# Sinkhorn normalisation re-laid: one (batch, head, source block) per partition, row sums by a block matrix on TensorE

## The chip, the core and the metric

The kernel runs on one core of one Trainium2 chip. The metric is the device time in microseconds (us) of one execution, as the median of several runs. Work is done by TensorE (PE, with its weight loads shown apart as PEld), VectorE (DVE), ScalarE (ACT) and GpSimd (POOL); SyncE (SP) issues plain transfers, POOL issues the loads that cast from float32 to bfloat16, and all transfers share 16 DMA engines.

## What is computed

The reference, cut to what matters here:

```
# q, k, v: (4, 8, 768, 64); sort_net: (4, 8, 8, 8); block = 96
P = sort_net
for _ in range(5):
    P = exp(P - max(P, axis=-1))
    P = P / (sum(P, axis=-1) + 1e-9)     # over source blocks j, for each target block i
    P = P / (sum(P, axis=-2) + 1e-9)     # over target blocks i, for each source block j
k_sorted, v_sorted = P applied to the 8 blocks of k and of v, for each (batch, head)
attn = softmax(q_block @ k_sorted_block.T / 8)       # inside each block of 96 rows
x = (attn @ v_sorted_block), heads side by side      # 3072 x 512
out = (s * relu(x @ w_in)**2 + b) @ w_out            # 512 -> 2048 -> 512
```

There are 32 (batch, head) pairs, so sort_net is 32 matrices of 8 x 8, or 256 rows (batch, head, i) of 8 numbers.

## The kernel before

**Tiles and stages.** The output's 3072 rows are made as eight tiles t of 384 rows; tile t is half of batch t//2. For each tile the attention pieces (`s_piece` for the scores and their exponential, `p_piece` for attention times values and the division, `t_piece` or a transposing DMA for turning x) feed `ffn1` (x times w_in, ReLU, square) and `ffn2` (times w_out, scale and bias). The order on every engine is the order of the program text: the schedule is written out by hand, and `Queue` drops small pieces into the slots of `ffn1` and `ffn2`. After the start-up the two feed-forward stages keep TensorE occupied to the end.

**The start-up.** Before the first `ffn1` can run, the following has to happen, in the program's order. SP loads `sn` (sort_net, 32 partitions of 64 numbers), then two broadcast scalars `s_bc` and `b_bc` (128 partitions of one number each), which are only used much later. POOL issues the loads of batch 0 in the order k, first half of q, v, second half of q (`load_k`, `load_q`, `load_v`), then builds constants (`ident`, `emat`, `bmask`, `hmask`), and then issues w_in, v of batch 1, w_out, and so on. TensorE meanwhile runs 82 matmuls of zeros (`warm_up`, L182), which do no work on the data. DVE and ACT run Sinkhorn on `sn` (L191 to L211): in each of the five rounds one exponential on ACT and then six or seven short DVE instructions, each of which needs the one before. ACT also writes zeros into the padding columns 96 to 127 of `vb` (`zero_pad`).

**From P to the mixing matrix.** `block_rows(g)` (L220) spreads the 32 matrices over 128 partitions, one partition per (batch, head, j), by a float32 matmul with `emat` and a masked sum on DVE, once for batches 0 and 1 (g = 0) and once for batches 2 and 3 (g = 1). `build_pd1` multiplies the result into a block-diagonal bfloat16 matrix `pd1`; `build_pd2` does so for `pd2`, in the middle of `ffn1(1)`.

**First consumers.** `q_half(0, "s")` transposes the first half of q on TensorE (tile `tq`, 48 transposes, L254) and ACT copies it out. Then `k_piece` (tile `tk`, L294) and `v_piece0` (tile `tv`, L320) mix k and v with `pd1`; their results are copied out of PSUM alternately by DVE ("v", L238) and ACT ("s", L240). The large PSUM tiles come from the pool `psa` (three buffers, shared by tq, tk, tv, scores and others), the small ones from `psb` (two buffers). Then come the four `s_piece` of tile 0, the `p_piece` with five further pairs of zero matmuls and `t_piece` among them, and `ffn1(0)` (tile `hps`, L459).

Of the kernel before, what the change touches and what calls it, by code (L numbers as in the profile page):

```python
# [9 lines left out]
FP = mybir.dt.float32  # L10
BF = mybir.dt.bfloat16
AF = mybir.ActivationFunctionType
ALU = mybir.AluOpType
AX = mybir.AxisListType
# [4 lines left out]
def kernel(  # L19
# [12 lines left out]
    nc = tc.nc  # L32

    B, H, S, D = q.shape
    NB = sort_net.shape[-1]
    BLK = S // NB
# [31 lines left out]
    ctx.enter_context(tc.manual_schedule())  # L68


    sn = sk.tile([BH, NB, NB], FP)
    nc.sync.dma_start(out=sn, in_=sort_net.rearrange("b h i j -> (b h) i j"))

    kb = const.tile([128, BLK, D], BF)
    vb = const.tile([128, 128, D], BF)
# [2 lines left out]
    def load_q(b, part=slice(0, 128)):  # L78


        if b == B - 1:
            qr[b] = qrp.tile([128, TQ, H, D], BF, tag="qr", name=f"qr{b}")
            for t in range(TQ):
                nc.gpsimd.dma_start(
                    out=qr[b][:, t],
                    in_=q[b][:, t * 128:(t + 1) * 128, :].rearrange("h p d -> p h d"))
            return
        if b not in qr:
            qr[b] = qrp.tile([128, H, TQ, D], BF, tag="qr", name=f"qr{b}")
        nc.gpsimd.dma_start(  # L90
            out=qr[b][part].rearrange("p h t d -> p h (t d)"),
            in_=q[b].rearrange("h (p t) d -> p h (t d)", t=TQ)[part])

    def load_k(rows, prow, n=1):
        for c0 in range(0, BLK, BLK // n):
            cs = slice(c0, c0 + BLK // n)
            nc.gpsimd.dma_start(out=kb[prow, cs, :], in_=kraw[rows, cs, :])

    def load_v(rows, prow):
        nc.gpsimd.dma_start(out=vb[prow, 0:BLK, :], in_=vraw[rows])  # L100

    def brows(b):
        return slice(b * 64, (b + 1) * 64), slice((b % 2) * 64, (b % 2) * 64 + 64)
# [12 lines left out]
    def new_vs(b):  # L116
# [4 lines left out]
    new_vs(1)  # L121
    nc.scalar.activation(out=warm, in_=warm, func=AF.Exp)

    load_k(*brows(0))
    load_q(0, slice(0, 64))
    load_v(*brows(0))
    load_q(0, slice(64, 128))


    ident = const.tile([128, 128], BF)  # L130
    make_identity(nc, ident)
    emat = const.tile([BH, 2 * 128], FP)
    nc.gpsimd.memset(emat, 1.0)
    nc.gpsimd.affine_select(out=emat, in_=emat, pattern=[[1, 2 * 128]], base=0,
                            channel_multiplier=-NB, compare_op=ALU.is_ge, fill=0.0)
    nc.gpsimd.affine_select(out=emat, in_=emat, pattern=[[-1, 2 * 128]], base=NB - 1,
                            channel_multiplier=NB, compare_op=ALU.is_ge, fill=0.0)
    bmask = const.tile([128, 16, NB], FP)
    nc.gpsimd.memset(bmask, 1.0)
    nc.gpsimd.affine_select(out=bmask, in_=bmask, pattern=[[-NB, 16], [0, NB]], base=0,  # L140
                            channel_multiplier=1, compare_op=ALU.is_ge, fill=0.0)
    nc.gpsimd.affine_select(out=bmask, in_=bmask, pattern=[[NB, 16], [0, NB]], base=NB - 1,
                            channel_multiplier=-1, compare_op=ALU.is_ge, fill=0.0)

    hmask = const.tile([128, H, NB], FP)
    nc.gpsimd.tensor_tensor(out=hmask, in0=bmask[:, 0:H], in1=bmask[:, H:2 * H], op=ALU.add)

    wis, wos = [], []
    NW = 2
# [29 lines left out]
    def warm_up(n, pool=psb):  # L179
        wp = pool.tile([128, 256], FP, tag="b" if pool is psb else "a", name="wp")  # L180
        for _ in range(n):
            nc.tensor.matmul(out=wp, lhsT=zt[:, 0:128], rhs=zt, start=True, stop=True)  # L182

    def zero_pad(r0):
        nc.scalar.copy(out=vb[:, r0:r0 + 16, :],
                       in_=zt[:, 0:D].unsqueeze(1).broadcast_to([128, 16, D]))


    rstat = sk.tile([BH, NB], FP)
    rrec = sk.tile([BH, NB], FP)  # L190
    nc.vector.tensor_reduce(out=rstat, in_=sn, axis=AX.X, op=ALU.max)  # L191
    nc.vector.tensor_tensor(out=sn, in0=sn, in1=rstat.broadcast_to([BH, NB, NB]),
                            op=ALU.subtract)
    between = [lambda: zero_pad(BLK), lambda: zero_pad(BLK + 16), lambda: None,
               lambda: None, lambda: None]
    for it in range(5):
        nc.scalar.activation(out=sn, in_=sn, func=AF.Exp)
        between[it]()
        nc.vector.tensor_reduce(out=rstat, in_=sn, axis=AX.X, op=ALU.add)
        nc.vector.reciprocal(out=rrec, in_=rstat)  # L200
        nc.vector.tensor_tensor(out=sn, in0=sn, in1=rrec.broadcast_to([BH, NB, NB]),
                                op=ALU.mult)
        nc.vector.tensor_reduce(out=rstat, in_=sn.rearrange("p i j -> p j i"),
                                axis=AX.X, op=ALU.add)
        if it == 0:
            nc.vector.tensor_scalar(out=rstat, in0=rstat, scalar1=1e-9, scalar2=None,
                                    op0=ALU.add)
        nc.vector.reciprocal(out=rrec, in_=rstat)
        cbc = bass.AP(tensor=rrec.tensor, offset=rrec.offset,
                      ap=[list(rrec.ap[0]), [0, NB], list(rrec.ap[1])])  # L210
        nc.vector.tensor_tensor(out=sn, in0=sn, in1=cbc, op=ALU.mult)  # L211
        if it == 2:
            nc.vector.tensor_reduce(out=jsel, in_=ident.rearrange("p (m x) -> p x m", x=NB),
                                    axis=AX.X, op=ALU.add)

    def bcast(t, n):
        return bass.AP(tensor=t.tensor, offset=t.offset,
                       ap=[list(t.ap[0]), [0, n], list(t.ap[1])])

    def block_rows(g):  # L220

        pe = psb.tile([128, 512], FP, tag="b", name="pe")
        nc.tensor.matmul(out=pe[:, 0:NB * NB], lhsT=emat[:, g * 128:(g + 1) * 128],
                         rhs=sn.rearrange("p i j -> p (i j)"), start=True, stop=True)
        tmp = sk.tile([128, NB, NB], FP, name=f"tmp{g}")
        nc.vector.tensor_tensor(out=tmp, in0=pe[:, 0:NB * NB].rearrange("p (i j) -> p i j", j=NB),
                                in1=bcast(jsel, NB), op=ALU.mult)
        pt = sk.tile([128, NB], FP, name=f"pt{g}")
        nc.vector.tensor_reduce(out=pt, in_=tmp, axis=AX.X, op=ALU.add)
        return pt  # L230


    pd1 = const.tile([128, 2, NHP, NB], BF)
# [10 lines left out]
    def q_half(half, eng):  # L244

        if half == 0:
            QT[0] = qtp.tile([128, NHP, S], BF, tag="qt", name="qt0")
        pr = slice(half * 64, half * 64 + 64)
        ps = psa.tile([128, 2, 1024], BF, tag="a", name="tq")
        for hp in range(NHP):  # L250
            for t in range(TQ):
                c0 = (hp % 2) * TG + t * 64
                for e in range(2):
                    nc.tensor.transpose(out=ps[e * 64:(e + 1) * 64, hp // 2, c0:c0 + 64],  # L254
                                        in_=qr[0][pr, 2 * hp + e, t, :], identity=ident[pr, pr])
        for a in range(2):
            evac(QT[0][:, 2 * a:2 * a + 2, half * TG:(half + 1) * TG].rearrange(
                     "q b (p t) -> q b p t", t=TQ),
                 ps[:, a, 0:2 * TG].rearrange("q (b t p) -> q b p t", b=2, t=TQ), eng)
# [53 lines left out]
    def v_piece0(d0, n, eng):  # L313

        if n > 8:
            ps = psa.tile([128, n, 64], FP, tag="a", name="tv")
        else:
            ps = psb.tile([128, n, 64], FP, tag="b", name="tv")
        for t in range(n):
            nc.tensor.matmul(out=ps[:, t, :], lhsT=vb[0:64, :, d0 + t],  # L320
                             rhs=pd1[0:64].rearrange("p e m i -> p (e m i)"),
                             start=True, stop=True)
        evac(VS[0][:, :, d0:d0 + n], ps[0:BLK].rearrange("p t g -> p g t"), eng)
# [226 lines left out]
        flush()  # L550

    def build_pd1():
        pt = block_rows(0)
        nc.vector.tensor_tensor(
            out=pd1, in0=hmask.rearrange("p (m e) i -> p e m i", e=2),
            in1=bass.AP(tensor=pt.tensor, offset=pt.offset,
                        ap=[list(pt.ap[0]), [0, 2], [0, NHP], list(pt.ap[1])]),
            op=ALU.mult)

    def build_pd2():  # L560
        pt2 = block_rows(1)
        for e in range(2):
            nc.vector.tensor_tensor(
                out=pd2[:, :, e],
                in0=bmask.rearrange("p (b m e) i -> p e b m i", b=2, e=2)[:, e],
                in1=bass.AP(tensor=pt2.tensor, offset=pt2.offset,
                            ap=[list(pt2.ap[0]), [0, 2], [0, NHP], list(pt2.ap[1])]),
                op=ALU.mult)


    warm_up(82)
    build_pd1()
    q_half(0, "s")
    k_piece(0, 0, 16, 1, "v")()
    k_piece(0, 32, 16, 1, "s")()
    k_piece(0, 64, 8, 1, "v")()
    k_piece(0, 80, 8, 1, "s")()
    v_piece0(0, 16, "v")
    v_piece0(16, 16, "s")
    v_piece0(32, 16, "v")  # L580
    s_piece(0, 0)
# [116 lines left out]
```

## Time and profile before

| What | Value |
|---|---|
| median of 5 runs | 237.13 us (236.83 to 237.71) |
| the profiled execution's own time | 237.25 us |
| span of that execution, first to last instruction | 235.6 us |
| TensorE busy | 226.2 us (96% of the span) |
| DVE, ACT, POOL busy | 125.5, 111.3, 43.8 us |
| mean granted TensorE clock | 0.971 of full speed |
| first `ffn1` matmul starts | 28.84 us into the span |
| first `k_piece` matmul starts | 14.41 us into the span |

Busy times come from one profiled execution, whose own time is 1.65 us more than its span. A busy TensorE is not a TensorE at its peak. A DMA's time to landing is counted from its issue. The line numbers (L182 and so on) are those of the kernel before.

### The profile page before, as it was taken

How to read it: one execution, taken by the hardware profiler on the slowest of the kernel's cores; microseconds unless marked ns; L12 is line 12 of the kernel's file. 1: busy time of each engine (PE TensorE's matmuls, PEld its weight loads, DVE VectorE, ACT ScalarE, POOL GpSimd, SP SyncE). 2: the span in 40 equal slices, each digit the busy share in tenths (PEclk: the TensorE clock that was granted, in tenths of full speed). 3: DMA queues.
4: the chain of work that ended last, by engine and by line, in shares of the span. 5: the costliest groups of instructions: out<-in, count | busy, mean ns of one | idle time of the engine just before them, and what ended most of it. 6: DMA issues, size and time to landing. Idle time of an engine off the chain costs nothing.

```text
span 235.6 us, 4923 instructions
## 1 busy us (share of the span) xinstructions
PE 226.2 (96%) x2072; PEld 138.1 (59%) x2090; DVE 125.5 (53%) x259; ACT 111.3 (47%) x163; POOL 43.8 (19%) x57
## 2 busy tenths in 40 slices
PE   8969999999999999999999999999999999999994
PEld 5859797765544555555555455656554556654443
DVE  5758655647993558866334744444362544442221
ACT  6158369775138441577776221656422226660000
POOL 7810000199960000394000000000000000000000
PEclk9985599999999999999999999999999999999999
DMA  5799999997799996499992415420024162001122
GB/s 91 113 206 214 225 192 205 228 218 166 115 128 204 263 310 155 114 112 104 128 61 93 111 45 131 94 67 4 0 93 108 51 111 45 0 0 47 58 76 89
DMA packets 38230, 28.11 MB, mean 119 GB/s; under 512 B 26432, under 2 KB 32576, under 8 KB 37696
## 3 DMA queue, kind: packets, MB, share of 16 engines
q0 software_dynamic: 13600, 15.21, 45.0%
q1 hardware_dynamic: 24464, 12.53, 23.2%
q8 instruction: 16, 0.26, 0.4%
q10 hardware_dynamic: 144, 0.07, 0.1%
q14 instruction: 6, 0.05, 0.1%
HBM read 29.63 MB, written 8.65 MB: 163 GB/s over the span
## 4 chain that ended last, share of the span: by engine, by line
PE 83%; DVE 6%; DMA 5%; ACT 2%; issue 1%; POOL 0%; POOLq 0%
PE hps L459 35%; PE ops L502 31%; DMA qr<-in_q_dram 5%; PE pv L402 4%; PE sc L375 3%; DVE gt L464 2%; DVE ks L238 2%; PE tv L320 2%; PE tk L294 2%; PE ops L487 1%; ACT ks L240 1%; PE tv L350 1%; PE tq L269 1%; PE tq L254 1%; PE tv L336 1%
## 5 line engine op out<-in xcount | busy, mean ns | idle before, releaser
L459 PE MATMUL hps<-xt,wi 128*128 128x384 bf16 (+1 forms) x576 | 88.2, 309 | 0.5 <-ACT rt L463 0.3
L502 PE MATMUL ops<-wo,gt 128*128 128x512 bf16 x350 | 83.7, 379 | 1.6 <-issue 1.0
L463 ACT ACTIVATE rt<-hps 128x768 bf16<-128x768 f32 (+1 forms) x72 | 53.2, 740 | 49.3 <-PE hps L459 48.1
L459 PEld LDWEIGHTS <-wi 128*128 128x128 bf16 x576 | 53.6, 98 | 30.6 <-issue 1.8
L464 DVE TENSOR_TENSOR gt<-rt 128x768 bf16<-128x768 bf16 (+1 forms) x72 | 41.1, 573 | 46.5 <-ACT rt L463 46.1
L502 PEld LDWEIGHTS <-gt 128*128 128x128 bf16 x368 | 33.7, 98 | 37.0 <-issue 0.6
L378 ACT ACTIVATE at<-sc 96x768 bf16<-96x768 f32 x32 | 24.4, 803 | 30.5 <-PE sc L375 30.5
L476 DVE SCALAR_TENSOR_TENSOR ot<-ops,s_bc,bias 128x512 f32<-128x512 f32 x23 | 17.2, 749 | 40.4 <-PE ops L502 40.3
L407 DVE TENSOR_TENSOR x<-pv,rec 96x512 bf16<-96x512 f32 (+1 forms) x36 | 22.6, 628 | 1.3
L238 DVE CAST ks<-tk 64x512 bf16<-64x512 f32 (+1 forms) x32 | 18.1, 565 | 2.0 <-PE tk L294 1.5
L240 ACT CAST ks<-tk 64x512 bf16<-64x512 f32 (+1 forms) x32 | 16.0, 500 | 6.4 <-PE tk L294 6.1
L623 POOL TENSOR_TENSOR csum<-csum,wo 128x512 f32<-128x512 f32 x14 | 17.6, 1255 | 1.0
L182 PE MATMUL wp<-zt 128*128 128x256 bf16 x92 | 14.4, 320 | 1.1 <-DVE warm L113 1.1
L402 PEld LDWEIGHTS <-at 96*128 96x128 bf16 (+1 forms) x256 | 12.0, 104 | 3.8
L402 PE MATMUL pv<-vs,at 96*128 96x66 bf16 (+1 forms) x256 | 13.0, 199 | 0.1
L375 PEld LDWEIGHTS <-ks 64*96 64x96 bf16 x256 | 8.4, 128 | 6.5 <-issue 5.7
L182 PEld LDWEIGHTS <-zt 128*128 128x128 bf16 x92 | 9.9, 113 | 3.2 <-DVE warm L113 1.1
L240 ACT CAST vn<-tv 128x512 bf16<-128x512 f32 (+1 forms) x12 | 9.4, 800 | 4.6 <-PE tv L350 3.9
L375 PE MATMUL sc<-qt,ks 64*96 64x96 bf16 x256 | 10.9, 219 | 0.6 <-DVE ks L238 0.5
L406 DVE RECIPROCAL rec<-pv 96x8 f32<-96x8 f32 (+1 forms) x36 | 6.9, 192 | 7.4 <-PE pv L402 7.4
L294 PEld LDWEIGHTS <-kb 64*128 64x128 bf16 x192 | 6.3, 95 | 4.5 <-issue 4.0
L294 PE MATMUL tk<-pd,kb 64*128 64x64 bf16 x192 | 7.9, 191 | 0.0
(70 smaller groups left out, 102.8 us busy)
## 6 DMA issues: line engine op xcount, KB each, us to landing
out_dram<-ot SPq DMA_DIRECT2D x23, 256.0 KB, 2.1
kb<-in_k_dram POOLq DMA_DIRECT2D x4, 768.0 KB, 10.9
vb<-in_v_dram POOLq DMA_DIRECT2D x4, 768.0 KB, 20.1
wi<-in_moe_w_in_dram POOLq DMA_DIRECT2D x2, 1024.0 KB, 20.7
wo<-in_moe_w_out_dram POOLq DMA_DIRECT2D x2, 1024.0 KB, 33.2
qr<-in_q_dram POOLq DMA_DIRECT2D x2, 768.0 KB, 27.0
dv<-vn SPq DMA_DIRECT2D x6, 256.0 KB, 8.0
vs<-dv POOLq DMA_DIRECT2D x4, 384.0 KB, 11.9
```

The lines of the kernel that those rows point to most:

```text
L182: nc.tensor.matmul(out=wp, lhsT=zt[:, 0:128], rhs=zt, start=True, stop=True)
L238: nc.vector.tensor_copy(out=out, in_=in_)
L240: nc.scalar.copy(out=out, in_=in_)
L294: nc.tensor.matmul(out=ps[:, c, :], lhsT=kb[pr, c0 + 2 * c:c0 + 2 * c + 2, :].rearrange("p c d -> p (c d)"), rhs=rhs, start=True, stop=True)
L375: nc.tensor.matmul(out=sc[:, e, n * BLK:(n + 1) * BLK], lhsT=ks[pr, g0 + n, :], rhs=QT[b][pr, hp, q0:q0 + BLK], start=True, stop=True)
L378: nc.scalar.activation(out=at, in_=sc[:, :, 0:TG], func=AF.Exp, scale=scale)
L402: nc.tensor.matmul(out=pv[e][0:m, (n - n0) * VW:(n - n0 + 1) * VW], lhsT=atf[:, c0:c0 + m], rhs=VS[b][:, gi, :], start=True, stop=True)
L407: nc.vector.tensor_tensor(out=x[:, n0:n0 + nn, hp * 128:(hp + 1) * 128].rearrange("p n (e d) -> p e n d", e=2), in0=pvv[:, :, :, 0:D], in1 ...
L459: nc.tensor.matmul(out=hps[:, f, 0:nt], lhsT=wi_at(hp, f0 + f), rhs=xt_at(t, hp, n0, nn), start=(hp == 0), stop=(hp == NHP - 1))
L463: nc.scalar.activation(out=rt[:, :, 0:nt], in_=hps[:, :, 0:nt], func=AF.Relu)
L464: nc.vector.tensor_tensor(out=gt[:, f0:f0 + 2, c0:c0 + nt], in0=rt[:, :, 0:nt], in1=rt[:, :, 0:nt], op=ALU.mult)
L502: nc.tensor.matmul(out=ops, lhsT=gt[:, f, m * 128:(m + 1) * 128], rhs=wo_at(f), start=(f == 0), stop=(f == NF - 1))
```

## The change

Sinkhorn is laid out anew. Two tiles `sn[0]` and `sn[1]` of 128 partitions and 8 numbers take the 256 rows of sort_net, by two loads. `sk_first(g)` subtracts the row maximum and expands the tile into a block-diagonal 128 x 128 matrix, and one float32 matmul with `jsel` turns it so that partition (batch, head, j) holds the 8 numbers of its i. From then on the sum over j is a sum over the 8 partitions of a block, which a float32 matmul with the block matrix `blk` gives on all 8 partitions at once; the sum over i lies within a partition and comes out of the same DVE instruction as the division (`accum_out`); its reciprocal `CC` is not multiplied in but handed to the next exponential as its per-partition scale. The later rounds leave out the maximum, as before. The two groups g = 0 and g = 1 take turns on the engines, and the zero matmuls are fewer and stand between the steps. `emat`, `block_rows` and `zero_pad` go away; the padding of `vb` is zeroed by POOL; the order of POOL's work and loads changes; `q_half(0, "s")` moves behind the first `v_piece0`.

```diff
-    sn = sk.tile([BH, NB, NB], FP)
-    nc.sync.dma_start(out=sn, in_=sort_net.rearrange("b h i j -> (b h) i j"))
+    snr = sort_net.rearrange("b h i j -> (b h i) j")
+    sn = []
+    for g in range(2):
+        t = sk.tile([128, NB], FP, name=f"sn{g}")
+        nc.sync.dma_start(out=t, in_=snr[g * 128:(g + 1) * 128])
+        sn.append(t)
...
-    load_k(*brows(0))
-    load_q(0, slice(0, 64))
-    load_v(*brows(0))
-    load_q(0, slice(64, 128))
     ident = const.tile([128, 128], BF)
     make_identity(nc, ident)
-    emat = ...                                   # memset and two affine_select on POOL
+    load_k(*brows(0))
     bmask = const.tile([128, 16, NB], FP)        # memset and two affine_select on POOL
...
+    load_v(*brows(0))
+    load_q(0, slice(0, 64))
+    nc.gpsimd.memset(vb[:, BLK:128, :], 0.0)
+    load_q(0, slice(64, 128))
     hmask = ...                                  # one tensor_tensor on POOL, now in pd1's order
...
-    def zero_pad(r0): ...
-    ... Sinkhorn on sn, L189 to L214, and block_rows, L216 to L230 ...
+    bm16 = const.tile([128, 16], FP)
+    nc.vector.tensor_reduce(out=bm16, in_=ident.rearrange("p (m x) -> p m x", x=NB),
+                            axis=AX.X, op=ALU.add)
+    nc.vector.tensor_reduce(out=jsel, in_=ident.rearrange("p (m x) -> p x m", x=NB),
+                            axis=AX.X, op=ALU.add)
+    blk = bmask.rearrange("p m x -> p (m x)")
+
+    def sk_first(g):
+        mx = sk.tile([128, 1], FP, name=f"mx{g}")
+        nc.vector.tensor_reduce(out=mx, in_=sn[g], axis=AX.X, op=ALU.max)
+        ex = sk.tile([128, 16, NB], FP, name=f"ex{g}")
+        nc.vector.scalar_tensor_tensor(
+            out=ex, in0=sn[g].unsqueeze(1).broadcast_to([128, 16, NB]), scalar=mx,
+            in1=bm16.unsqueeze(2).broadcast_to([128, 16, NB]), op0=ALU.subtract, op1=ALU.mult)
+        W[g] = psb.tile([128, 512], FP, tag="b", name="w")
+        nc.tensor.matmul(out=W[g][:, 0:NB], lhsT=ex.rearrange("p m x -> p (m x)"), rhs=jsel,
+                         start=True, stop=True)
...
+    def sk_step(g, it):
         if it == 0:
+            nc.scalar.activation(out=E[g], in_=W[g][:, 0:NB], func=AF.Exp)
+        else:
+            nc.scalar.activation(out=E[g], in_=Y[g], func=AF.Exp, scale=CC[g])
+        r = psb.tile([128, 512], FP, tag="b", name="r")
+        nc.tensor.matmul(out=r[:, 0:NB], lhsT=blk, rhs=E[g], start=True, stop=True)
+        nc.vector.reciprocal(out=rr[:, g], in_=r[:, 0:NB])
+        nc.vector.scalar_tensor_tensor(out=Y[g], in0=E[g], scalar=1.0, in1=rr[:, g],
+                                       op0=ALU.mult, op1=ALU.mult, accum_out=cs[:, g:g + 1])
+        if it == 0:
+            ...                                  # tensor_scalar: cs + 1e-9
+        nc.vector.reciprocal(out=CC[g], in_=cs[:, g:g + 1])
...
     def build_pd1():
-        pt = block_rows(0)
-        ...                                      # one tensor_tensor: hmask * pt
+        ...                                      # one scalar_tensor_tensor: Y[0] * CC[0] * hmask
     def build_pd2():
-        pt2 = block_rows(1)
+        pt2 = sk.tile([128, NB], FP, name="pt2")
+        nc.vector.tensor_scalar(out=pt2, in0=Y[1], scalar1=CC[1], scalar2=None, op0=ALU.mult)
         ...                                      # two tensor_tensor, as before
...
-    warm_up(82)
-    build_pd1()
-    q_half(0, "s")
+    warm_up(9, psa)
+    sk_first(0)
+    warm_up(2, psa)
+    sk_first(1)
+    for it in range(5):
+        sk_step(0, it)
+        if it == 4:
+            build_pd1()
+        warm_up(3, psa)
+        sk_step(1, it)
+        warm_up(3, psa)
     k_piece(0, 0, 16, 1, "v")()
     k_piece(0, 32, 16, 1, "s")()
     k_piece(0, 64, 8, 1, "v")()
     k_piece(0, 80, 8, 1, "s")()
     v_piece0(0, 16, "v")
+    q_half(0, "s")
     v_piece0(16, 16, "s")
```

More of the change, by code (lines that the diff above doesn't have):

```diff
@@ L122 @@
     nc.scalar.activation(out=warm, in_=warm, func=AF.Exp)
-    load_k(*brows(0))
-    load_q(0, slice(0, 64))
-    load_v(*brows(0))
-    load_q(0, slice(64, 128))
     ident = const.tile([128, 128], BF)
     make_identity(nc, ident)
[L132 to L137, printed above, removed]
+    load_k(*brows(0))
     bmask = const.tile([128, 16, NB], FP)
@@ L143 @@
                             channel_multiplier=-1, compare_op=ALU.is_ge, fill=0.0)
-    hmask = const.tile([128, H, NB], FP)
-    nc.gpsimd.tensor_tensor(out=hmask, in0=bmask[:, 0:H], in1=bmask[:, H:2 * H], op=ALU.add)
+    load_v(*brows(0))
+    load_q(0, slice(0, 64))
+    nc.gpsimd.memset(vb[:, BLK:128, :], 0.0)
+    load_q(0, slice(64, 128))
+    hmask = const.tile([128, 2, NHP, NB], FP)
+    nc.gpsimd.tensor_tensor(out=hmask.rearrange("p e m i -> p m e i"),
+                            in0=bmask[:, 0:H].rearrange("p (m e) i -> p m e i", e=2),
+                            in1=bmask[:, H:2 * H].rearrange("p (m e) i -> p m e i", e=2),
+                            op=ALU.add)
     wis, wos = [], []
@@ L182, in warm_up @@
             nc.tensor.matmul(out=wp, lhsT=zt[:, 0:128], rhs=zt, start=True, stop=True)
[L184 to L204, printed above, removed]
-        if it == 0:
[L206 to L230, printed above, removed]
+    bm16 = const.tile([128, 16], FP)
@@ new lines @@
+    nc.vector.tensor_reduce(out=bm16, in_=ident.rearrange("p (m x) -> p m x", x=NB),
[3 more added lines that the diff above has]
+    blk = bmask.rearrange("p m x -> p (m x)")
+    E, Y, CC, W = {}, {}, {}, {}
+    def sk_first(g):
[8 more added lines that the diff above has]
+                         start=True, stop=True)
+        E[g] = sk.tile([128, NB], FP, name=f"e{g}")
+        Y[g] = sk.tile([128, NB], FP, name=f"y{g}")
+        CC[g] = sk.tile([128, 1], FP, name=f"cc{g}")
@@ new lines @@
+    rr = sk.tile([128, 2, NB], FP)
+    cs = sk.tile([128, 2], FP)
+    def sk_step(g, it):
+        if it == 0:
+            nc.scalar.activation(out=E[g], in_=W[g][:, 0:NB], func=AF.Exp)
[7 more added lines that the diff above has]
+        if it == 0:
+            nc.vector.tensor_scalar(out=cs[:, g:g + 1], in0=cs[:, g:g + 1], scalar1=1e-9,
+                                    scalar2=None, op0=ALU.add)
+        nc.vector.reciprocal(out=CC[g], in_=cs[:, g:g + 1])
@@ L552, in build_pd1 @@
     def build_pd1():
-        pt = block_rows(0)
[L554 to L558, printed above, removed]
+        y = Y[0]
+        nc.vector.scalar_tensor_tensor(
+            out=pd1.rearrange("p e m i -> p (e m) i"),
+            in0=bass.AP(tensor=y.tensor, offset=y.offset,
+                        ap=[list(y.ap[0]), [0, H], list(y.ap[1])]),
+            scalar=CC[0], in1=hmask.rearrange("p e m i -> p (e m) i"),
+            op0=ALU.mult, op1=ALU.mult)
     def build_pd2():
-        pt2 = block_rows(1)
+        pt2 = sk.tile([128, NB], FP, name="pt2")
+        nc.vector.tensor_scalar(out=pt2, in0=Y[1], scalar1=CC[1], scalar2=None, op0=ALU.mult)
         for e in range(2):
```

## The prediction

> **What bounds the kernel now.** I read the page first, then the chain of waits up to 75 us, the timelines of DVE, PE and SP over the first 30 us, the DMA issues with their landings, and the granted clock in short windows. The page:
>
> ```profile
> PE   8969999999999999999999999999999999999994
> PEclk9985599999999999999999999999999999999999
> ```
>
> One digit is 5.9 us. From the sixth digit on PE is full. So what the change does to the start-up passes on to the end: the first `ffn1` matmul stands at 28.84 us, and whatever it moves by, the end moves by. The clock's only gap is in digits 3 to 5. The chain of waits through the start-up:
>
> ```profile
> 1.98 11.51 DMA qr<-in_q_dram
> ...
> 13.53 0.96 PE tq L254 x48
> ...
> 14.52 1.50 ACT qt L240 x2
> 16.02 0.63 ACT ks L240
> ...
> 19.00 3.01 PE tv L320 x32
> 22.01 0.36 PE sc L375 x7
> ```
>
> Not Sinkhorn but the first half of q ends last, at 13.49 us. Sinkhorn is as late, though; DVE's timeline has one round and its end:
>
> ```profile
> 5.31 0.21 DVE L199 TENSOR_REDUCE rstat<-sn 32x8 f32<-32x64 f32 x1 [0.32 <-ACT sn L197]
> ...
> 12.79 0.23 DVE L226 TENSOR_TENSOR tmp<-pe,jsel 128x64 f32<-128x64 f32 x1 [0.71 <-PE pe L223]
> 13.05 0.22 DVE L229 TENSOR_REDUCE pt<-tmp 128x8 f32<-128x64 f32 x1
> 13.38 0.22 DVE L554 TENSOR_TENSOR pd<-hmask,pt 128x64 bf16<-128x64 f32 x1
> ```
>
> The step 199 recurs at 5.31, 7.12, 8.88 and 10.65: a round lasts 1.77 us, 0.32 of it the passage through ACT; a float32 matmul costs DVE 0.71 of waiting. `pd1` is there at 13.60, 0.1 us after q. Both gates must move for a gain. The third gate is v, seen in PE's timeline, and then the transfers of the start:
>
> ```profile
> 14.41 1.62 PE L294 MATMUL tk<-pd,kb 64*128 64x64 bf16 x48
> 17.20 1.61 PE L320 MATMUL tv<-pd,vb 64*128 64x64 bf16 x16 [1.17 <-issue]
> ```
>
> ```profile
> kb<-in_k_dram POOLq DMA_DIRECT2D x1, 768.0 KB, 7.4
> sn<-in_sort_net_dram SPq DMA_DIRECT2D x1, 8.0 KB, 1.6
> s_bc<-in_moe_s_dram SPq DMA_DIRECT2D x1, 0.5 KB, 9.1
> ```
>
> v is issued at 2.68 and takes 14.4 us, landing at 17.1, where tv starts. The last fence is the one to remember: `sn`, 32 rows, landed in 1.6 us; `s_bc`, issued 0.47 us later with 128 rows, in 9.1, because k began between them. From 4 to 7 us the DMA view counts 41 packets of POOL's queue and 41 of SP's: they alternate one for one, and k's packets are 12 KB each (0.50 MB in 41).
>
> **The change, part by part.** The sum is made against the profiled execution, 237.25 us (0.12 above the median of the runs).
>
> *Start of Sinkhorn.* ACT's first exponential starts at 2.94. After: `ident` must exist (its POOL steps took 0.61 from 3.89 to 4.50; from about 0.8 they end at 1.4), two masked sums over it (L213: 0.36 each, to 2.2), `sn[0]` lands (2.45 as now), maximum 0.21, expansion 128x128 (no row of that size: between 0.23 for 128x64 and 0.36 for L213; 0.30), matmul 0.71. That gives 3.8: 0.9 later.
>
> *A round.* Passage through ACT 0.32, matmul 0.71 with its waits, then reciprocal 0.19, division with sum (0.21 to 0.26 like L211, with a possible second step for the sum), reciprocal 0.19, gaps 0.03 each: 1.75, as long as now. But PE works in order, and between two uses by one group stand the other group's matmul and six zero matmuls. Zero matmuls cost 0.108 at full speed (62 from 5.6 to 12.3 us) and twice that, 0.213, at half. With 0.43 for each of two float32 matmuls (L223) PE needs 1.5 us a round at full clock, so the chain rules, or 2.1 at half, so PE rules.
>
> *Which clock?* Clock by windows:
>
> ```profile
> 12.40:15.70 3.30, 2.52 (x94) 1.00 0.98 197
> 15.90:19.20 3.30, 1.94 (x22) 0.50 1.18 204
> 22.60:26.00 3.40, 3.29 (x49) 0.50 1.11 211
> 26.00:29.40 3.40, 3.18 (x28) 0.50 1.21 242
> 29.50:33.00 3.50, 3.50 (x52) 1.00 1.01 181
> ```
>
> Columns: PE busy and count, clock, DMA. The clock fell at 15.8 after 3.4 us of quarter- and half-array matmuls (tq, tk) with the longest pause 0.78 us, and stayed down while PE was busy 3.29 of 3.40 us, until the zero pairs came close together. Sinkhorn's new filling, 6 x 0.213 of 2.1 us, is 61% of full-array work: between the stretch that did not raise the clock and the one that did. I take it as half and half, so 1.95 us a round.
>
> The Trainium skill, "TensorE: Matmul & The Clock Gate", in its table of why this matters, asks only for no pause over some 3 us between bursts. This trace shows the clock fall without one; by the page alone the new loop would keep full speed and the sum would be the faster rival's.
>
> *First k matmul (now 14.41).* First r at 4.3 (behind the second group's W), the fifth four rounds later: 4.3 + 4 x 1.95 = 12.1, and 0.2 for the 1e-9 step, partly hidden. After it PE still has three zero matmuls, the other group's r and three more, a round: 14.2 us (13.4 at full clock, 14.9 at half). `pd1`, 0.43 + 0.9 + 0.25 after the r, is ready by then. tk no longer waits for tq. So -0.2, from -1.0 to +0.5; k landed at 8.7 and hides.
>
> *q behind v_piece0.* The queue is k, v, q instead of k, q, v. k and v then land by about 13, and q where v did, 17.1 plus 0.2 for the ident steps ahead of k. tq waits besides for one of three psa buffers, free when DVE has copied the first tk, about 3.5 after tk's start, 17.7. On ACT the 1.50 of qt moves from ahead of the copies of k, where ACT waited for tk anyway, to behind them. ACT starts some 1.2 after tk instead of 0.1: at `s_piece(0, 0)` I charge 0.7 (0.4 to 1.0, the upper end with tk at half clock, since 16 of them then take 0.85 instead of 0.53). The wait of 1.17 for v goes, but what is late next is ACT, so I credit nothing.
>
> *POOL.* `emat` (0.32, 0.41, 0.39) goes; a memset of 128x2048 comes between the q loads: from 128x128 (0.24) and 32x256 (0.32), some 1 ns an element, 2 us. w_in's issue moves from 7.15 to about 7.7, but its queue is backed up until q lands, so it hides. If that cover were gone it would cost 0.5. Cover to watch: the second half of w_in lands 31.45, is used at 32.58. A gain over 1.1 us at `ffn1` is taken back there. `zero_pad` (2 x 1.03) lay in ACT's waits for DVE: nothing.
>
> *build_pd2, mid-kernel.* The matmul at 55.26 held PE 0.36 (next hps at 55.62): gone. DVE loses tmp and pt (0.15 and 0.23 on the chain) and gains one 128x8 step (0.2 to 0.3), in a stretch where PE later waits 0.47 for DVE. Credit 0.4 (0.3 to 0.8).
>
> Sum: -0.2 + 0.7 - 0.4 = +0.1, so 237.35; I give 237.4. Bounds: -1.0 + 0.4 - 0.8 = -1.4 and +0.5 + 1.0 - 0.3 = +1.2.
>
> **Rivals.**
>
> *The second Sinkhorn load is stuck behind k (slower).* `sn[1]`, 128 rows, is issued at about 1.4, where `s_bc` was. DVE has its maximum, and PE its W, ahead of everything in `sk_step`, so both groups wait for it. If k's first packets come before its own, it gets one small packet for each 12 KB one. Then it lands at 1.4 + 9.1 = 10.5 if it fares like `s_bc`, and about 13.5 if v's big packets follow k's where q's small ones did: 8 rows and a completion per engine against 4 + 4 packets of k and v at 1.1 to 1.3 us. DVE wants it at 3.1; beyond that point each us counts: +7.4 to +10.4. Against it: `ident` now precedes k on POOL, so k starts 0.1 to 0.5 us later. For it: `s_bc` got no packet in before k. 244.8 to 247.8; I take 246.5.
>
> The Trainium skill, "DMA: Bandwidth & Descriptors", section on queues, rings and completion order, says that a DMA engine takes turns between queue rows packet by packet, and that a packet holds typically 9 to 17 descriptors. By that, the 8 rows of an engine would pass behind a single packet of k, for 1 to 2 us; the 41 against 41, and 9.1 us for `s_bc`, show row for packet, which speaks against this change, and the price above goes by them.
>
> *The clock stays at full speed (faster).* Then -1.0 + 0.4 - 0.6 = -1.2: 236.0. For it: eleven matmuls of zeros at the start; against it: the 61%.
>
> *Sinkhorn is bound by cold zero matmuls (slower).* 2.1 us a round or a little more, tk at 15, +0.6 to +0.9, with +1.0 and -0.3: 238.7.
>
> **How the numbers follow.** A measurement here can tell 0.2%, 0.47 us, from no change. Forecast (237.4, within 236.5 to 238.1): 0.32. Sn[1] late: 0.33. Full clock: 0.22. Cold: 0.13. Faster by over 0.2%: the full clock's 0.22 and 0.03 of the forecast, 0.25. Same: 0.15 of the forecast. Slower: the rest, 0.60. The range reaches from 236.0 to 247.8, over both outer cases, since each is more than 0.2; the forecast's own is 236.5 to 238.1.
>
> **What would show it.** Right: exponentials 0.9 later at the start, rounds of 1.75 to 2.1 us, first tk at 13.4 to 14.9 with no wait for q, ACT's qt after its copies of k, no float32 matmul near 55 us. The rival: a landing of 9 us or more on an `sn` load, and DVE idle until then. Wrong altogether: PE idle after 30 us, at w_in or v of batch 1.

## The result and the profile after

The changed kernel takes 237.93 us (median of 36 runs) against 237.4 us of the kernel before, run beside it on the same chips (71 runs). The ratio is 1.002, 95% interval 1.0011 to 1.0029: 0.5 us slower, at the edge of the 0.2% that can be told from no change. Six of the 36 runs, the profiled one among them, took 241.5 to 245.7 us, against one of the 71; the ratio leaves these out, and what brings them about is open. A second measurement, `e1_again` below, gave 1.0014 (0.9999 to 1.003). The forecast was 237.4, and its range held the result. But two of its three terms were wrong by 0.6 to 0.8 us, in opposite directions: that the sum came so near is luck.

The profile taken with the first measurement was disturbed from 80 us on by a late landing of v of batch 1, so it is read only up to 71 us; the rest is read from a second profile of the same kernel (238.64 us, span 236.7).

PE's row in the second profile's page, its clock, and the last chain by engine:

```profile
PE   8999999999989999999999999999999999999994
PEclk9999999999999999999999999999999999999999
...
PE 81%; DMA 9%; POOL 5%; DVE 2%; issue 1%; ACT 0%
```

PE is full as before, with one weaker digit at 65 to 71 us. The chain now runs for 9% of the span through a transfer and for 5% through GpSimd (POOL): those two shares are what the prediction did not see. The clock row must not be taken at its word: it shows 9 where the records hold no change of the clock, and the durations of the matmuls contradict it. First the second profile's PE timeline:

```profile
13.62 2.74 PE L288 MATMUL tk<-pd,kb 64*128 64x64 bf16 x48
16.17 1.57 PE L314 MATMUL tv<-pd,vb 64*128 64x64 bf16 x16
17.90 1.49 PE L248 MATMUL tq<-ident,qr 64*64 64x64 bf16 x48 [0.16 <-DVE ks L232]
```

and the first profile's:

```profile
13.40 1.56 PE L288 MATMUL tk<-pd,kb 64*128 64x64 bf16 x48 [0.17 <-DVE rr L218]
17.35 1.49 PE L248 MATMUL tq<-ident,qr 64*64 64x64 bf16 x48 [0.88 <-DVE ks L232]
```

The same 48 matmuls take 1.56 us in one execution and 2.74 in the other: in the first the clock was up when k came, in the second it stayed at half through the whole start. The kernel before, with its 82 dense matmuls of zeros, took 1.62. In both profiles tk comes 0.8 to 1.0 us earlier than before (14.41), with no wait for q; tq comes some 4 us after tk, behind the copies of k, on PE and on ACT:

```profile
15.54 4.80 ACT L234 CAST ks<-tk 64x512 bf16<-64x512 f32 x8 [3.15 <-PE tk L288]
20.36 1.50 ACT L234 COPY qt<-tq 128x768 bf16<-128x768 bf16 x2
```

The two `sn` loads, with the small load that the large rival was priced by (DMA issues of the first 6 us, second profile):

```profile
sn<-in_sort_net_dram SPq DMA_DIRECT2D x2, 4.0 KB, 1.7
s_bc<-in_moe_s_dram SPq DMA_DIRECT2D x1, 0.5 KB, 11.8
```

Each half of `sn` landed in 1.7 us, so the rival that was given 0.33 is refuted; `s_bc` still took 11.8.

To follow where the time goes, the span is cut at marks read from the timelines of PE, ACT and DVE: the first k matmul (tk); the first `ffn1` matmul; the first `rt`, ACT's first step of `ffn1`; the 24th `rt`, just behind the place of `build_pd2`; the first and the sixth `ot`, DVE's output evictions; the end. Starts in us, then lengths:

| kernel | tk | first ffn1 | first rt | to 24th rt | on to first ot | on to sixth ot | on to the end |
|---|---|---|---|---|---|---|---|
| before | 14.41 | 28.84 | 29.98 | 29.76 | 11.35 | 22.15 | 142.32 |
| changed, second profile | 13.62 | 29.23 | 30.50 | 29.28 | 12.03 | 22.64 | 142.25 |
| changed, first profile | 13.40 | 28.71 | 30.02 | 29.28 | 12.04 | | |
| e2: before, pd2's matmul early | 14.46 | 28.77 | 29.62 | 29.29 | 11.82 | 23.38 | 142.32 |
| e5: changed, q of batch 2 first | 13.61 | 29.26 | 30.28 | 29.28 | 12.06 | 22.15 | 142.23 |
| e6: before, q of batch 2 first | 14.41 | 28.75 | 29.61 | 29.76 | 11.37 | 22.15 | 142.32 |
| e7: e6 and e2 together | 14.54 | 28.83 | 29.69 | 29.29 | 11.86 | 22.15 | 142.33 |
| e9: e6, half of the additions left out | 14.38 | 28.70 | 29.55 | 29.76 | 10.77 | 27.96 | 142.83 |
| e10: e9 and e2 together | 14.36 | 29.13 | 29.98 | 29.30 | 10.77 | 24.90 | 142.82 |
| e11: before, q behind v at the start | 13.53 | 28.70 | 29.60 | 29.75 | 11.37 | 22.57 | 142.32 |
| e12: e5, pd2 built at 34.6 us | 13.60 | 29.23 | 30.50 | 29.29 | 10.77 | 22.15 | 142.25 |

Read down a column: apart from the three starts, and from e9 and e10, a length takes the same value to 0.1 us wherever the code of that stretch is the same and no transfer is waited for, so a difference of 0.2 us means something there. The first `rt` does not: e6, whose start is that of the kernel before, has it 0.37 earlier. In e6 the granted clock is back at full from 27.5 us on and the first eight `ffn1` matmuls take 0.82 us; before, it is back at 29.5 and they take 1.10. So a start is better read at the first `ffn1` matmul, where e6 and before are 0.09 apart. The second profile of the changed kernel is 1.14 us longer than before: +0.52 at the first `rt` (+0.39 at the first `ffn1` matmul), +0.20 in the middle (-0.48 and +0.68), +0.49 before the sixth `ot`, -0.07 after it. The middle's +0.20 is in both profiles; the other two vary from run to run.

### The profile page after: what moved, and what is told of

It reads as the page before. It is cut to its first block, busy times and chain, and to the rows that moved or that the text cites. A ratio compares the mean times of both kernels' runs of the same rounds, so it can differ in the third digit from the quotient of the medians.

```text
span 241.6 us, 4916 instructions
## 1 busy us (share of the span) xinstructions
PE 230.0 (95%) x2051; PEld 139.9 (58%) x2069; DVE 125.1 (52%) x270; ACT 110.9 (46%) x166; POOL 44.7 (19%) x55
## 4 chain that ended last, share of the span: by engine, by line
PE 79%; DMA 15%; DVE 3%; issue 1%; ACT 0%; SPq 0%; DVEq 0%
PE hps L453 30%; PE ops L496 29%; DMA vs<-dv 8%; DMA dv<-vn 8%; PE pv L396 4%; PE wp L183 4%; PE sc L369 3%; PE tv L314 2%; PE tk L288 2%; PE ops L481 1%; DVE ks L232 1%; PE r L217 1%; PE tq L248 1%; PE tq L263 1%; PE tv L344 1%
## 5 line engine op out<-in xcount | busy, mean ns | idle before, releaser
L496 PE MATMUL ops<-wo,gt 128*128 128x512 bf16 x350 | 85.3, 385 | 1.8 <-issue 1.2
L458 DVE TENSOR_TENSOR gt<-rt 128x768 bf16<-128x768 bf16 (+1 forms) x72 | 40.2, 561 | 46.6 <-ACT rt L457 46.2
L396 PEld LDWEIGHTS <-at 96*128 96x128 bf16 (+1 forms) x256 | 12.8, 109 | 7.1 <-issue 4.0
L396 PE MATMUL pv<-vs,at 96*128 96x66 bf16 (+1 forms) x256 | 13.8, 205 | 2.9 <-DMA vs<-dv 2.8
L183 PE MATMUL wp<-zt 128*128 128x256 bf16 x51 | 13.4, 400 | 1.1 <-DVE warm L117 1.1
L183 PEld LDWEIGHTS <-zt 128*128 128x128 bf16 x51 | 7.0, 163 | 2.1 <-DVE warm L117 1.1
```

The costliest lines, as they stand in the source:

```text
L396: nc.tensor.matmul(out=pv[e][0:m, (n - n0) * VW:(n - n0 + 1) * VW], lhsT=atf[:, c0:c0 + m], rhs=VS[b][:, gi, :], start=True, stop=True)
L458: nc.vector.tensor_tensor(out=gt[:, f0:f0 + 2, c0:c0 + nt], in0=rt[:, :, 0:nt], in1=rt[:, :, 0:nt], op=ALU.mult)
L496: nc.tensor.matmul(out=ops, lhsT=gt[:, f, m * 128:(m + 1) * 128], rhs=wo_at(f), start=(f == 0), stop=(f == NF - 1))
```

## The experiments

Each was timed in five rounds beside the kernel before (`e8_k_first` in one).

**e1_again**: the changed kernel as it is, for a second profile.

> The changed kernel once more, nothing edited, for a second trace and a narrower interval. Theory A (the rounds of Sinkhorn run at half the granted clock, bound by their zero matmuls, and the half clock then lasts through the consumers up to about 29 us): first k matmul at 13.2 to 13.6 us, first ffn1 matmul within 0.3 us of 28.84, time 0.1 to 0.7 us above the kernel before. Theory B (the 0.4 us credited in mid-kernel is not there, or is given back later): the first ffn1 matmul is not later than before, and the half microsecond is lost behind 40 us.

Measured: 237.78 us, ratio 1.0014 (0.9999 to 1.003); its lines are above. Neither theory holds alone: the first `ffn1` matmul is 0.39 later, a little more than theory A allowed, and the other half of the loss comes behind 30 us. The wait for q, as the view of PE's waits from 57 to 105 us has it:

```profile
PE sc L369 <- DVE ks L232: 0.5, 1, 0.5
PE bps L540 <- DVE ks L232: 0.4, 1, 0.4
PE tq L263 <- DMA qr<-in_q_dram: 0.4, 1, 0.4
```

Only the first of these three stood in the kernel before. The last is q of batch 2, issued by GpSimd at 68.24 behind the additions and the loads of k, landing at 90.16, 21.9 us later. Before, it was issued at 67.64, landed 21.1 later, at 88.74, and was used at 88.99.

### The start

**e4_no_zeros**: are rounds bound by the zero matmuls?

```diff
-        warm_up(3, psa)
         sk_step(1, it)
-        warm_up(3, psa)
```

> The changed kernel without the 30 zero matmuls inside the five rounds (the eleven ahead of them stay). If the zero matmuls bind the rounds, a round falls from 1.76 to 1.5 to 1.65 us and the first k matmul comes at 12.6 to 13.0 us; the clock is then at half from the start to about 29 us in every run, and the 48 k matmuls take 2.6 us instead of 1.5, so that the first ffn1 matmul stays within 0.4 us of the changed kernel's. If the clock in the start-up did not matter, since copies bind there, ffn1 and the end would come 0.5 to 0.8 us earlier than in the changed kernel.

Measured: 237.81 us, ratio 1.0016 (0.9996 to 1.0037). The first group's reciprocals, DVE's timeline:

```profile
6.86 0.21 DVE L218 RECIPROCAL rr<-r 128x8 f32<-128x8 f32 x1 [0.31 <-PE r L217]
...
8.66 0.21 DVE L218 RECIPROCAL rr<-r 128x8 f32<-128x8 f32 x1 [0.35 <-PE r L217]
...
10.43 0.21 DVE L218 RECIPROCAL rr<-r 128x8 f32<-128x8 f32 x1 [0.35 <-PE r L217]
```

A round is 1.77 to 1.80 us without a single zero matmul, and in the changed kernel's second profile the same steps stand at 6.86 and 8.66. The chain rules, not PE: the zeros cost a round nothing, even at half clock. Behind the last round they do hold back tk, which here waits for `pd1` instead and starts at 13.33 rather than 13.62:

```profile
13.33 2.72 PE L288 MATMUL tk<-pd,kb 64*128 64x64 bf16 x48 [0.44 <-DVE pd L548]
```

That gain does not show in the time.

**e3_q_back**: the changed kernel with the old order of loads and q's transposition ahead of k's.

```diff
-    load_v(...); load_q(0, first half); memset; load_q(0, second half)
+    load_q(0, first half); load_v(...); memset; load_q(0, second half)
...
+    q_half(0, "s")
     k_piece(0, 0, 16, 1, "v")()
...
     v_piece0(0, 16, "v")
-    q_half(0, "s")
```

> The changed kernel with one part undone: load order k, q, v and the transposes of the first half of q ahead of the k pieces again. By the step of the prediction that charges 0.7 us for q behind v_piece0 and credits the earlier k, undoing it has tk wait for q: tk at 14.5 to 15.0 us instead of 13.4, the first ffn1 matmul 0 to 0.4 us later than in the changed kernel, time 0 to +0.5 us against it. If the move of q was a plain loss of 0.7 us, this is 0.3 us or more faster than the changed kernel.

Measured: ratio 1.007 (1.0042 to 1.0098), from four of its nine runs. Its start, PE's timeline:

```profile
13.91 1.49 PE L248 MATMUL tq<-ident,qr 64*64 64x64 bf16 x48 [0.23 <-DMA qr<-in_q_dram]
15.34 2.74 PE L288 MATMUL tk<-pd,kb 64*128 64x64 bf16 x48
```

tk came at 15.34, later than either theory had it: q landed at 13.9, and tq then took 1.49 of PE ahead of k. I had expected 0 to 0.5 us more than the changed kernel, or 0.3 less; it is 1.3 us worse in this kernel than `e1_again`, timed with it. With the old order tk stands behind q's landing and tq, however early the table is ready.

**e11_q_late**: the reverse, the kernel before with q last.

```diff
     load_k(*brows(0))
-    load_q(0, slice(0, 64))
     load_v(*brows(0))
+    load_q(0, slice(0, 64))
     load_q(0, slice(64, 128))
...
-    q_half(0, "s")
...
     v_piece0(0, 16, "v")
+    q_half(0, "s")
```

> The kernel before with only the order of the start changed as in the changed kernel: loads k, v, q, and q's transposition behind the first v piece. The clock is at full speed from 5.6 us in this kernel. Theory (the order k, v, q costs what q's late landing costs, and that is 0.4 to 1.0 us between the first k matmul and ffn1): tk at 13.6 to 13.7 as the table is ready at 13.60, first ffn1 matmul at 28.4 to 29.1, the time within 0.3 us of before. Rival (the order is what makes the changed kernel slow, whatever the clock): first ffn1 matmul at 29.2 or later, the time 0.4 us or more above before.

Measured: 237.52 against 237.17 us, ratio 1.0005 (0.9991 to 1.0019). PE's timeline:

```profile
13.53 1.56 PE L294 MATMUL tk<-pd,kb 64*128 64x64 bf16 x48 [0.91 <-DVE pd L554]
14.93 1.62 PE L320 MATMUL tv<-pd,vb 64*128 64x64 bf16 x16
17.38 1.49 PE L254 MATMUL tq<-ident,qr 64*64 64x64 bf16 x48 [0.83 <-DVE ks L238]
```

tk moved to the table's 13.5, and the first `ffn1` matmul stood at 28.70, against 28.75 to 28.84 in e6 and before. Some 0.9 us gained at tk, 0.1 of it left. So q's new place costs 0.7 to 0.8 us by `ffn1` in a kernel whose clock is up when k comes, and the earlier tk is worth no more than that. tk, tv and tq stand here at the times of the changed kernel's first profile, to 0.15 us; in the second profile tk lasts 1.2 us longer at half clock, and the first `ffn1` matmul is at 29.23 instead of 28.70.

**e8_k_first**: is the second `sn` load at risk when k is issued earlier?

```diff
+    load_k(*brows(0))
     ident = const.tile([128, 128], BF)
     make_identity(nc, ident)
-    load_k(*brows(0))
```

> The changed kernel with the load of k issued first on POOL again, ahead of the two steps that make ident. Rival of the prediction (the second Sinkhorn load is stuck behind k's large packets): sn[1] lands at 9 us or later instead of at 3.0, DVE waits for it, the first k matmul comes at 20 us or later, and the time is 6 to 10 us longer. If k's start does not decide: sn[1] lands within 0.5 us of the changed kernel's, and the time is within 0.5 us.

Measured: 237.96 us, ratio 1.0033 (1.0017 to 1.0049). DMA issues of the first 6 us:

```profile
kb<-in_k_dram POOLq DMA_DIRECT2D x1, 768.0 KB, 7.4
...
sn<-in_sort_net_dram SPq DMA_DIRECT2D x2, 4.0 KB, 1.8
s_bc<-in_moe_s_dram SPq DMA_DIRECT2D x1, 0.5 KB, 8.2
```

Still 1.8 us. Here the two issues of `sn` take SP from 0.81 to 1.69, and k is issued at 1.31. In the kernel before, `s_bc` was issued at 1.28 with k at 1.31, and took 9.1. Standing in the same place against k, one small load was late and the other not: my reading of `s_bc` as "128 rows queued against k" was wrong. What sets it apart (4 bytes a row against 32, for one) was not tried. What this kernel loses goes with `ident`, which came later, and with it tk, at 14.20.

### The middle

**e2_pd2_early**: build_pd2's credit alone, in the kernel before: the float32 matmul, tmp and pt are done at the start.

```diff
+    PT2 = []
     def build_pd2():
-        pt2 = block_rows(1)
+        pt2 = PT2[0]
...
     build_pd1()
+    PT2.append(block_rows(1))
```

> The kernel before with one part alone: the float32 matmul and the two DVE steps that make the matrix of batches 2 and 3 move from the middle of ffn1(1) to the start, behind build_pd1, where PE waits for q. If the credit of 0.4 (0.3 to 0.8) us for that part is right, this is 0.3 to 0.8 us faster than the kernel before. If DVE or a landing takes the place of the matmul in the 55 to 70 us stretch (theory B), it is within 0.1 us of the kernel before.

Measured: 237.63 us, ratio 1.0004 (0.9989 to 1.002): nothing. In the table the 0.47 us is gained by the 24th `rt` and all lost by the first `ot`: 29.29 + 11.82 = 41.11, as before (29.76 + 11.35). And the wait for q of batch 2 is there as well, longer:

```profile
PE tq L269 <- DMA qr<-in_q_dram: 1.2, 1, 1.2
```

**e5_q2_after, e6_q2_before, e7_q2_pd2**: q of batch 2 is issued ahead of k of batches 2 and 3, in the changed kernel, in the kernel before, and in the latter together with e2's edit.

```diff
-    seq(load_k(2), load_k(3), load_q(2), bias_piece)
+    seq(load_q(2), load_k(2), load_k(3), bias_piece)
```

> The changed kernel with one edit of order: at the middle of the kernel POOL issues the load of q of batch 2 ahead of the two loads of k (batches 2 and 3), not behind them. Theory P (the time of both kernels is pinned near 90 us by the landing of that q, so that what is saved ahead of it is waited for there): the wait of PE for q at about 90 us (0.4 us in the last trace of the changed kernel) is gone, q lands 5 us or more earlier, and the time falls by 0.4 to 1.2 us against the changed kernel. Theory W (the wait is only where a loss elsewhere shows, or the k loads take q's place as the late ones): within 0.2 us of the changed kernel.

> The same edit of order in the kernel before: q of batch 2 ahead of k of batches 2 and 3. Theory P: PE reaches q there just as it lands (0.2 us apart in the trace), so 0 to 0.4 us is gained. With the pin gone in both, the changed kernel with this edit should be faster than this one by what the prediction credited, 0.3 us or a little more. Theory W: within 0.2 us of the kernel before, and no difference between the two.

> The kernel before with two edits: the matrix of batches 2 and 3 made at the start (which alone moved nothing) and q of batch 2 loaded ahead of k. Theory P: the 0.4 us credited for the float32 matmul and two DVE steps now shows, so this is 0.3 to 0.8 us faster than the kernel before with the q edit alone. Theory W, or DVE taking the matmul's place for good: no more than 0.15 us apart.

Measured: 237.67 us (1.0008; 0.9994 to 1.0022), 237.04 (0.9992; 0.9981 to 1.0003) and 237.25 (0.9994; 0.9978 to 1.001). The wait is gone in all three, and the stretch to the sixth `ot` is 22.15 in each. That is worth at most 0.3 us, less than theory P had for e5. And e5 was to be faster than e6, but is 0.6 us slower; e7 was to be faster than e6 by the credit, and it is not: what swallows the credit lies ahead of the first `ot`.

What it is stands in DVE's timeline beside GpSimd's. In e6, build_pd2's steps and what follows:

```profile
57.11 0.21 DVE L226 TENSOR_TENSOR tmp<-pe,jsel 128x64 f32<-128x64 f32 x1
57.35 0.22 DVE L229 TENSOR_REDUCE pt<-tmp 128x8 f32<-128x64 f32 x1
57.61 0.81 DVE L563 TENSOR_TENSOR pd<-bmask,pt 128x64 bf16<-128x64 f32 x2
58.34 4.37 DVE L464 TENSOR_TENSOR gt<-rt 128x768 bf16<-128x768 bf16 x3
```

In e7, without the first two:

```profile
57.19 1.31 DVE L565 TENSOR_TENSOR pd<-bmask,pt 128x64 bf16<-128x64 f32 x2
58.43 4.36 DVE L464 TENSOR_TENSOR gt<-rt 128x768 bf16<-128x768 bf16 x3
...
55.68 10.59 POOL L626 TENSOR_TENSOR csum<-csum,wo 128x512 f32<-128x512 f32 x8
```

The last line is GpSimd's: eight additions for the bias, 1.3 us each, back to back. The gt steps take 1.45 us each beside them and 0.56 where GpSimd adds nothing. With tmp and pt gone, the two pd steps take as much longer, and gt starts at 58.43 instead of 58.34. DVE goes at GpSimd's pace there; work taken from it becomes waiting. In the changed kernel's second profile:

```profile
57.98 1.12 DVE L557 TENSOR_SCALAR pt<-y,cc 128x8 f32<-128x8 f32 x1
59.14 1.32 DVE L559 TENSOR_TENSOR pd<-bmask,pt 128x64 bf16<-128x64 f32 x2
60.38 3.40 DVE L458 TENSOR_TENSOR gt<-rt 128x768 bf16<-128x768 bf16 x3
```

The one 128x8 step that the prediction charged with 0.2 to 0.3 us takes 1.12. build_pd2 holds DVE for 2.40 us (57.98 to 60.38) instead of 1.23. The Trainium skill, "SBUF — State Buffer", section "Who interferes with whom", sorts these steps: VectorE and GpSimd share a pair of ports, held for a whole instruction; an operation with two inputs in SBUF needs it (gt, pd), so can a tensor_scalar from SBUF to SBUF (the new step), and a reduction never does (pt), nor, outside the two-port modes, one with a single SBUF input (tmp, whose other operand is in PSUM). All five rows here agree: tmp and pt keep 0.21 and 0.22 us beside the additions, and gt, pd and the new step grow to 1.45, 0.81 to 1.32 and 1.12. By that rule the change replaces two free steps by one that queues.

**e9_half_csum, e10_half_csum_pd2**: e6 and e7 without the second eight additions.

```diff
     load_v(*brows(3))
-    csums(8, NF)
```

> The kernel before, q of batch 2 issued ahead of k (as in e6_q2_before), and without the second eight of GpSimd's additions for the bias: that part of the sum over w_out is left out of the output. Theory (the stretch from 55 to 66 us goes at GpSimd's pace, VectorE's steps there being locked to the additions): VectorE's gt steps there fall from 1.5 us to 0.6 and PE's waits near 67 us go; 0.3 to 0.8 us faster than e6, 236.3 to 236.8. Rival (the additions cost VectorE nothing that anyone waits for): as e6, 237.0.

> The same, and the table's float32 matmul and its VectorE steps for batch 1 done at the start (as in e7_q2_pd2). Theory (the locked stretch swallowed the 0.4 us that the earlier matmul saves): now the saving stays, 0.3 to 0.5 us faster than e9_half_csum, and the first ffn1 matmul as there. Rival (the 0.4 us is swallowed by something else, such as PE's later wait for ks, or was never on the path): no faster than e9.

Measured: 241.94 us (ratio 1.0167; 1.0124 to 1.0209) and 241.71 (1.017; 1.0136 to 1.0204): as times, both expectations missed by 5 us. Up to the first `ot` the theory held. e9's steps on DVE:

```profile
56.27 0.22 DVE L226 TENSOR_TENSOR tmp<-pe,jsel 128x64 f32<-128x64 f32 x1
...
56.77 0.36 DVE L563 TENSOR_TENSOR pd<-bmask,pt 128x64 bf16<-128x64 f32 x2
57.55 0.56 DVE L464 TENSOR_TENSOR gt<-rt 128x768 bf16<-128x768 bf16 x1 [0.42 <-ACT rt L463]
```

pd falls from 0.81 to 0.36 and gt from 1.45 to 0.56; from the first `rt` to the first `ot` e9 takes 40.53 us and e10 40.07: on this stretch the credit is there, 0.46 us. (The first `ot` itself is no earlier, 70.05 against 70.08, as e10's first `ffn1` matmul came 0.43 later, which was not expected.) But the additions had also kept GpSimd from issuing the loads of batch 2. GpSimd's timeline, then PE's waits in e9:

```profile
55.51 0.90 POOL L90 DMA_DIRECT2D qr<-in_q_dram  x1
56.40 0.53 POOL L97 DMA_DIRECT2D kb<-in_k_dram  x1
```

```profile
PE pv L402 <- DMA vs<-dv: 4.0, 1, 4.0
```

q and k of batch 2 start at 55.5 and 56.4 instead of 66.1 and 67.0, run beside the transfers of v of batch 1, and PE waits 4.0 us for that v (2.6 in e10). That these loads made v late is argued, not shown: the first profile of the changed kernel has the same wait, of 2.8 us, with q issued at 67.76, behind the additions.

**e12_pd2_ahead**: nothing left out. The changed kernel with q of batch 2 first, and build_pd2 called where DVE is idle and GpSimd adds nothing.

```diff
-                   lambda: q_half(1, "s"), ...
+                   seq(lambda: q_half(1, "s"), build_pd2), ...
...
-    ffn1(1, Queue([nothing] * 4 + [build_pd2] + [nothing] * 3, 8))
+    ffn1(1, Queue([nothing] * 8, 8))
```

> The changed kernel, q of batch 2 issued ahead of k (as in e5_q2_after), and the three VectorE steps of build_pd2 moved from 57 us, beside GpSimd's additions, to about 34.5 us, where VectorE is idle for 1.9 us. Nothing is left out. Theory (beside the additions these steps last 2.44 us, of which some 0.4 is work, and that gives back the 0.47 us of the float32 matmul and 0.2 more): the steps last 0.4 to 0.6 us there; PE's waits for VectorE's ks at 67 and 70 us shrink; from the first ffn1 matmul to the first output eviction 41.4 to 41.9 us instead of 42.36 in e5; the time 0.5 to 0.9 us under e5's 237.67, 236.8 to 237.2, at or under the kernel before. Rival (VectorE stays locked to GpSimd's additions until 67 us whatever it has to do, so a step less frees nothing): 42.3 again, 237.6.

Measured: 236.46 us (235.79 to 236.91) against 237.43, ratio 0.9955 (0.994 to 0.997): 1.1 us faster than the kernel before by the ratio, and below the 236.8 that was the lower end of what was expected; the changed kernel took 237.8 to 237.9. The three steps:

```profile
34.61 0.22 DVE L557 TENSOR_SCALAR pt<-y,cc 128x8 f32<-128x8 f32 x1
34.87 0.36 DVE L559 TENSOR_TENSOR pd<-bmask,pt 128x64 bf16<-128x64 f32 x2
```

1.12 us has become 0.22, 1.32 has become 0.36. In the table only one length differs from e5 beyond the first `rt`: 10.77 instead of 12.06. That is 1.29 us for 2.40 us of DVE steps, more than the 0.5 to 0.9 expected. DVE now catches up before the additions end, and then waits 0.15 us for PE's tk; PE waits for DVE nowhere from 57 to 105 us. The chain by engine has neither a transfer nor GpSimd left in it:

```profile
PE 95%; DVE 3%; issue 1%; ACT 0%
```

What the new layout of Sinkhorn has to do with this gain is not shown, since no run has the kernel before with these steps moved. e7, which has the old layout, would reach its sixth `ot` 0.8 us before e12 if its 11.86 became 10.77; that is an estimate from the table.

## Why the prediction was right and wrong

*The start of Sinkhorn*: right. The first exponential was expected at 3.8, and started at 3.73 and 3.79.

*A round*: 1.95 us was predicted, 1.77 to 1.80 measured at half clock. The step that failed is "2.1 at half, so PE rules". It charged each float32 matmul 0.43, its duration; but from its start to that of the zeros behind it are only 0.29 (11.71 to 12.01 in the second profile), and with three zeros, 0.6, PE needs 0.9 for one group, which is the chain's pace. *First k matmul*: so 13.4 to 13.6 instead of 14.2; the term was -0.8 to -1.0 and not -0.2, near the lower bound given.

*q behind v_piece0*: +0.7 (0.4 to 1.0) predicted. At full clock e11 gives 0.7 to 0.8: right. In the changed kernel tk to the first `ffn1` matmul is 15.31 and 15.61 us in its two profiles, against 14.34 to 14.43 with the start of before: 0.9 to 1.0 more with the clock up at tk, 1.2 to 1.3 with it at half. The upper end charged the half clock to 16 of the 48 k matmuls only (0.85 instead of 0.53). Together the two terms of the start came to -0.13 and +0.39 at the first `ffn1` matmul, where -0.2 + 0.7 = +0.5 was predicted: near in the second profile, by two errors in opposite directions.

*POOL*: right. PE has no wait for w_in; the new memset took 1.83 us, where 2 were predicted, and is hidden.

*build_pd2*: -0.4 predicted, +0.20 measured, in both profiles; 0.6 us less would have put the changed kernel at the time of the kernel before. That the matmul's 0.4 is gone was right (-0.48 at the 24th `rt`). That DVE "loses tmp and pt and gains one 128x8 step (0.2 to 0.3), in a stretch where PE later waits 0.47 for DVE" was wrong in its price: 0.22 is the step alone, 1.12 the step beside GpSimd. The rows to see it were in the profile of before: the wait of 0.47, quoted in the prediction itself, that showed DVE to be the late one, and the chain of waits, which leaves PE at 55.37 and stays on DVE from 56.21 to 70.28, with gt at 1.3 to 1.4 us a step:

```profile
56.21 1.32 DVE gt L464
...
58.76 4.29 DVE gt L464 x3
```

So the 0.36 us of PE was credited in a stretch that ran at DVE's pace.

*q of batch 2*: not in the sum. "PE idle after 30 us" was named as the sign of a wrong prediction, but for w_in or v; it came at q of batch 2, 0.42 us in one profile of the changed kernel and up to 1.15 in e2. A transfer that lands just in time before is a gate of its own for whatever arrives earlier or is issued later.

*The rivals.* `sn[1]` behind k: refuted, 1.7 us against the 9 or more charged. The 1 to 2 us that the prediction worked out from the Trainium skill, "DMA: Bandwidth & Descriptors", were nearer here than the row of `s_bc`, though e8 shows that the row was the wrong one to compare with rather than that the page's rule holds for `s_bc`. Cold zeros: refuted by e4. Full clock: half true. Of the changed kernel's 30 runs that enter the ratio, 18 read a mean clock of 0.999 or 1.000, like the second profile with its half-speed start, and have a median of 238.1; 12 read 0.97 to 0.98, and have 237.5, next to the 237.4 of the kernel before. Even these are not at 236.0: that rival's sum had -0.6 for the start, where the first profile shows -0.13, and -0.6 for the middle, where both show +0.20. In the second profile PE paused nowhere for more than 0.22 us from its first matmul to the end of the start, and the clock stayed at half all the same, so the absence of pauses is not enough.

*The chances.* Slower by over 0.2% was given 0.60, most of it for a rival that did not happen. The result is slower by just that bound, by a mechanism that was not among the rivals.

## What to carry to other kernels

Before crediting a step taken off an engine, look whether its neighbours in that stretch are slower than the same instructions elsewhere: where they are, the engine goes at another's pace, a step removed becomes waiting, and a step added can cost nearly a whole instruction of the other (1.12 us of 1.3 here). Then move the step rather than shorten it: on its stretch e12 gained 1.3 us by that, where e7's shorter chain gained nothing. And before taking work off a queue that also issues transfers, look which of them would then start earlier.

## What was not expected of the hardware

- GpSimd's additions may have acted as a brake that helped: without half of them two loads were issued 10.6 us earlier, PE waited 4.0 us for another transfer, and the time rose to 241.94 us (e9). That the one caused the other was not isolated.
- Whether the clock rises during the start differs between executions of one kernel: with the same zero matmuls it was up at the first k matmul in one profile (1.56 us) and at half in the other (2.74). The changed kernel sits at an edge that the dense filling of the kernel before does not touch; where the edge lies was not found.
- A division that also writes its sum issues a second instruction, DVE_READ_ACCUMULATOR, of 0.08 us; the range of 0.21 to 0.26 us for the pair covered it (0.17 + 0.08).
